# Inverting the softmax sums on Pool by a power of minus one, in place of DVE's reciprocal

## The chip, the cores and the metric

One core of a Trainium2 chip. The metric is the device time of one execution in microseconds (us), as the median of several runs.

Engine names are those of the profile: PE (matmul), PEld (weight load), DVE (VectorE), ACT (ScalarE), POOL (GpSimd), SP (the queue that issues the DMAs). L283 is line 283 of the kernel in question; the changed kernel's lines stand up to 5 higher than those of before.

## The reference

Attention with 32 inducing points over 4 batches of 12416 tokens of width 128, then a gated feed-forward layer (width 1536) on all 49664 tokens. Cut to what matters:

```python
def mab(q, kv):
    s = scale * (q @ kv.transpose(0, 2, 1))
    s = s - s.max(-1, keepdims=True)
    a = np.exp(s)
    a /= a.sum(-1, keepdims=True) + 1e-09      # the sums that the change inverts (second call)
    return a @ kv
h = mab(I, x)                                  # I: 32 inducing points
x = mab(x, h)                                  # each token: softmax over 32
...
ffn_out = gelu(x @ w_gate) * (x @ w_val) @ w_out
out = x + sigmoid(x @ w_res) * ffn_out
```

## The kernel before

Per batch there are 97 blocks of 128 tokens in 13 tiles of up to 8 blocks, and 25 token groups of 4 blocks (the last of 1). The exponentials of the second softmax lie in `e`, one block of 32 values per token, and their sums in `z`, a tile of up to 32 columns (one per block). Pool forms the sums, DVE inverts them, Pool multiplies to the normalised weights `a2`, and a DMA transposes these into `rt`, the right-hand side of all the products of that tile.

```python
p_sm = ... bufs=2                      # tag "a2": a ring of two buffers
p_fin ...                              # tags "th" and "at": rings of three, "fe": of two

def sums_b(b, j0, j1, eng):            # on Pool: halving additions in an a2 buffer
    t = p_sm.tile([P, PRE, Q, M], FP16, name="a2", tag="a2")...
    po.tensor_tensor(t[:, :w], ev[:, :, :M // 2], ev[:, :, M // 2:], AL.add)
    ...                                # three more halvings
    po.tensor_tensor(z.unsqueeze(2), t[:, :w, 0:1], t[:, :w, 1:2], AL.add)

def ones_b(b, j0, j1):
    z = e_of["z", b, t0][:, j0 - t0:j1 - t0]
    ve.reciprocal(z, z)

def weights_b(b, k, ...):
    a2 = p_sm.tile([P, PRE, Q, M], FP16, name="a2", tag="a2")
    eng.tensor_tensor(a2[:, :n], <e>, <z, broadcast>, AL.mult)
    sy.dma_start_transpose(rt, a2[:, :n]...)

def spread(b, c0, c1):                 # the next batch's first layer (h times w_gate, w_val), spread to hgv
    a2 = p_sm.tile([P, PRE, Q, M], BF16, name="a2", tag="a2")
    po.tensor_copy(a2[:, :n, 2 * s:2 * s + 2, :], hgt...)   # twice
    sy.dma_start_transpose(hgv_t[b]..., a2[:, :n]...)

def end(self, on_act):                 # the end of a token group
    if on_act:
        act.activation(fe, f, AC.Copy, bias=0.0, scale=1.0)
        po.tensor_tensor(th, th, fe, AL.mult)
        po.tensor_tensor(at, at, fe, AL.add)
    else:
        ve.scalar_tensor_tensor(th, th, 1.0, f, AL.add, AL.mult)
    po.tensor_tensor(at, at, th, AL.add)
    sy.dma_start(out[...], at)
```

The order in which all of this is queued stands in three tables of 25 rows, one row per token group: `plan_first`, `plan` (batches two and three) and `plan_last`. G is a half-slot of gates on PE and its gelu on ACT; V, Q, P a slot of values with none, one or two gates; a number the matmuls of the last layer; R and A the ACT instructions for `th` and `at`; E exponentials of the next batch, and behind the last of each block of 32 the sums; `o` a reciprocal; `l` one half of the next batch's first layer, after the second of which come the spread copies; a star an ending on ACT.

The softmax here doesn't subtract the row's maximum and nothing guards it: scores larger than these inputs give would overflow.

## Time and profile before

| | before |
|---|---|
| median of all its runs beside the changed kernel | 772.44 us (770.61 to 775.49, 6 runs) |
| ACT / DVE / PE busy, of a span of 770.5 us | 753.3 / 741.2 / 738.9 us |
| Pool busy | 467.4 us (61%) |
| reciprocals on DVE | 17, in sum 4.7 us |
| endings on ACT (fe) / on DVE (th) | 35 / 65 |

Three engines are nearly full, and Pool is at 61% only as an average. Between 77 and 116 us, where it also splits the next batch's input, it is busy for 35.5 of 39 us, and at the change to the third batch it works with hardly a gap from 380.6 to 397.1 us.

### The profile page before, as it was taken

To read this page: it belongs to the slowest core of one execution; us is meant where nothing else is said; L and a number is where in the kernel's file an instruction comes from. 1 tells how busy PE (TensorE), PEld (TensorE's weight loads), DVE (VectorE), ACT (ScalarE), POOL (GpSimd) and SP (SyncE) were. 2 spreads that over 40 slices of the span, in tenths; PEclk is the share of its full clock that TensorE was granted. 3 is DMA by queue.
4 is the path that set the end of the run, shared out by engine and by line. 5 is a ranking of instruction groups with operands and counts; after the bars stand their busy time and mean duration, and the time that the engine had idled before them with its cause. 6 is when DMAs were issued, how large, how long until landed. Compare 5 with 4: busy or idle time off the path is not lost.

```text
span 770.5 us, 23888 instructions
## 1 busy us (share of the span) xinstructions
PE 738.9 (96%) x9583; PEld 432.5 (56%) x9583; DVE 741.2 (96%) x735; ACT 753.3 (98%) x1506; POOL 467.4 (61%) x470
## 2 busy tenths in 40 slices
PE   6799999999999999999999999999999999999997
PEld 4455555565655655565655555556565555555555
DVE  7699999999999999989999999998999999999997
ACT  6899999999999999999999999999999999999997
POOL 0526988822787978923377797961367773443334
PEclk9889999999999999999999999999999999999999
DMA  8314589701055677521035496750105431110101
GB/s 340 124 45 129 134 191 188 165 30 43 31 119 110 157 176 192 141 46 43 29 65 112 112 210 154 139 150 29 39 21 128 87 88 43 42 43 29 42 30 60
DMA packets 118448, 78.15 MB, mean 101 GB/s; under 512 B 96672, under 2 KB 99392, under 8 KB 118336
## 3 DMA queue, kind: packets, MB, share of 16 engines
q1 hardware_dynamic: 118336, 76.62, 39.2%
q8 instruction: 75, 1.23, 0.7%
q14 instruction: 37, 0.30, 0.1%
HBM read 27.87 MB, written 25.43 MB: 69 GB/s over the span
## 4 chain that ended last, share of the span: by engine, by line
PE 47%; ACT 35%; issue 10%; DVE 4%; POOL 3%; DMA 1%; SPq 0%; ACTq 0%; DVEq 0%; POOLq 0%
ACT ge L368 23%; PE f L391 22%; PE g L357 12%; PE v L357 7%; PE g L399 3%; DVE u L362 3%; ACT at L410 3%; ACT th L405 3%; ACT e L166 2%; ACT fe L419 2%; ACT xt L141 1%; POOL lo L124 1%; ACT L166 1%; DMA xf<-in_x_dram 1%; DMA ge<-in_x_dram 1%
## 5 line engine op out<-in xcount | busy, mean ns | idle before, releaser
L362 DVE TENSOR_TENSOR u<-ge,v 128x1024 bf16<-128x1024 f32 x584 | 671.7, 1212 | 8.2 <-PE g L357 1.9
L368 ACT ACTIVATE ge<-g 128x512 f32<-128x512 f32 x1164 | 608.3, 661 | 2.7 <-PE g L357 1.6
L391 PEld LDWEIGHTS <-u 128*128 128x128 bf16 x4656 | 270.8, 98 | 206.3 <-issue 200.4
L391 PE MATMUL f<-wO,u 128*128 128x128 bf16 x4656 | 374.4, 221 | 4.0 <-DVE th L423 0.5
L357 PE MATMUL g<-rt,hgv 32*128 32x512 f16 x1152 | 337.7, 380 | 7.3 <-ACT ge L368 0.4
L357 PE MATMUL v<-rt,hgv 32*128 32x512 f16 x1152 | 222.3, 385 | 2.5 <-DVE u L362 1.5
L424 POOL TENSOR_TENSOR at<-at,th 128x512 f32<-128x512 f32 (+1 forms) x99 | 123.6, 1248 | 147.8 <-DVE th L423 66.1
L357 PEld LDWEIGHTS <-hgv 32*128 32x128 bf16 x2400 | 75.3, 91 | 87.8 <-issue 22.8
L420 POOL TENSOR_TENSOR th<-th,fe 128x512 f32<-128x512 f32 (+1 forms) x35 | 42.2, 1205 | 92.9 <-ACT fe L419 92.9
L294 POOL TENSOR_TENSOR a<-e,z 128x1024 f16<-128x1024 f32 (+1 forms) x48 | 89.8, 1880 | 5.7 <-DMA hgv<-a 5.4
L124 POOL TENSOR_TENSOR lo<-xf,hi 128x1024 f16<-128x1024 f32 x36 | 76.8, 2135 | 0.2
L399 PE MATMUL g<-hra,rt 128*128 128x128 f16 x768 | 72.1, 219 | 1.5
L410 ACT ACTIVATE at<-g 128x512 f32<-128x512 f32 (+1 forms) x100 | 65.0, 651 | 0.0
L405 ACT ACTIVATE th<-g 128x512 f32<-128x512 f32 (+1 forms) x100 | 64.3, 650 | 0.3 <-PE g L399 0.3
L399 PEld LDWEIGHTS <-rt 128*128 128x128 f16 x768 | 50.8, 98 | 12.4 <-issue 10.4
L423 DVE SCALAR_TENSOR_TENSOR th<-th,f 128x512 f32<-128x512 f32 (+1 forms) x65 | 44.1, 678 | 3.0 <-PE f L391 0.6
L118 POOL CAST hi<-xf 128x1024 f16<-128x1024 f32 x36 | 37.4, 1038 | 11.1 <-DMA xf<-in_x_dram 6.7
L421 POOL TENSOR_TENSOR at<-at,fe 128x512 f32<-128x512 f32 (+1 forms) x35 | 42.1, 1204 | 0.0
L162 PEld LDWEIGHTS <-xt 128*128 128x128 f16 x768 | 23.4, 97 | 7.2 <-issue 3.0
L166 ACT ACTIVATE e<-g 128x512 f32<-128x512 f32 (+3 forms) x40 | 20.4, 600 | 2.4 <-PE g L162 2.2
L419 ACT ACTIVATE fe<-f 128x512 f32<-128x512 f32 (+1 forms) x35 | 22.8, 650 | 0.0
L273 POOL TENSOR_TENSOR a<-a 128x256 f32<-128x256 f32 (+8 forms) x48 | 20.0, 416 | 3.8
(113 smaller groups left out, 261.0 us busy)
## 6 DMA issues: line engine op xcount, KB each, us to landing
out_dram<-at SPq DMA_DIRECT2D x96, 256.0 KB, 2.2
xf<-in_x_dram SPq DMA_DIRECT2D x38, 512.0 KB, 4.5
ge<-in_x_dram SPq DMA_DIRECT2D x10, 512.0 KB, 8.2
rt<-a SPq DMA_TRANSPOSE x48, 3.1
xt<-hi SPq DMA_TRANSPOSE x36, 4.2
ge<-in_moe_w_gate_dram SPq DMA_DIRECT2D x1, 512.0 KB, 9.3
ge<-in_moe_w_val_dram SPq DMA_DIRECT2D x1, 512.0 KB, 9.5
ge<-in_moe_w_out_dram SPq DMA_DIRECT2D x1, 512.0 KB, 4.9
```

What stands on the lines that cost most here:

```text
L124: eng.tensor_tensor(lo[:, :w, :P], xf_t.pop((b, k))[:, :w, :], hi_t[b, k][:, :w, :], AL.subtract)
L166: act.activation(e[:, (j0 - t0) * M:(j1 - t0) * M], bank[:, :(j1 - j0) * M], AC.Exp, bias=0.0, scale=scale)
L294: eng.tensor_tensor(a2[:, :n], ev[:, o:o + n, :].unsqueeze(2).to_broadcast([P, n, Q, M]), z[:, o:o + n].unsqueeze(2).unsqueeze(3).to_broad ...
L357: pe.matmul(*t[n], start=True, stop=True)
L362: ve.tensor_tensor(u[:, :n], ge_t.pop(value)[:, :n], v_t.pop(value)[:, :n], AL.mult)
L368: act.activation(ge_t[i][:, h * TOK:h * TOK + n], gb[:, :n], AC.Gelu, bias=0.0, scale=1.0)
L391: pe.matmul(self.ffn[:, k, :], u_t[self.gi, si][:, o:o + P], wO[:, fc, :], start=first, stop=not self.todo, skip_group_check=True)
L399: pe.matmul(bank[:, k * P:(k + 1) * P], rt_t[self.b, self.k][:, self.j0 + k, :], hra_t[self.b][:, s, :], start=True, stop=True)
L405: act.activation(self.th[:, :self.tw], self.mix(0), AC.Tanh, bias=0.0, scale=0.5)
L410: act.activation(self.at[:, :self.tw], self.mix(1), AC.Copy, bias=0.0, scale=1.0)
L423: ve.scalar_tensor_tensor(th, th, 1.0, f, AL.add, AL.mult)
L424: (ve if self.gi == ngrp - 1 else po).tensor_tensor(at, at, th, AL.add)
```

## The change

The intent is to take the reciprocals off DVE, one of the three full engines, and put them on Pool, the one with time left. The two earliest of the 17 stay on DVE. As Pool makes the sums itself, the inversion can follow at once and the `o` steps go from the tables. The tables were rearranged for that, so the change has two parts: the place of the inversion, and a new order of everything else.

```diff
-    def ones_b(b, j0, j1):
+    def ones_b(b, j0, j1, eng=po):
         z = e_of["z", b, t0][:, j0 - t0:j1 - t0]
-        ve.reciprocal(z, z)
+        if eng is ve:
+            ve.reciprocal(z, z)
+        else:
+            po.tensor_tensor(z, z, minus[:, :j1 - j0], AL.pow)
...
+    po.memset(minus, -1.0)
...
-                at(i, lambda j=j: sums_b(0, *j, po))
-                at(i + 6, lambda j=j: ones_b(0, *j))
+                at(i, lambda j=j: (sums_b(0, *j, po), ones_b(0, *j)))
...
                     sums_b(nb, j0 // WIDE * WIDE, j1, po)
+                    ones_b(nb, j0 // WIDE * WIDE, j1)
+                    inverted[nb] = j0 // WIDE * WIDE + WIDE
...   (the "o" step goes; all three tables are replaced; one row of each as an example)
-        "Q8G Q9 AGVr16 EEV VEEE2 EE11Q",
+        "RtQ2 GQ10A Qr20E EEV VEEEE 13P",
```

More of the change, by code (lines that the diff above doesn't have):

```diff
@@ L442 @@
     parts = konst.tile([P, 1], FP32, name="parts")
+    minus = konst.tile([P, WIDE], FP32, name="minus")
     sy.dma_start(ind_f, inducing)
@@ L522 @@
     sums_b(0, 0, half, ve)
-    ones_b(0, 0, half)
+    ones_b(0, 0, half, ve)
     sums_b(0, half, WIDE, po)
@@ L532 @@
     first_layer(0, TOK)
-    ones_b(0, half, WIDE)
+    ones_b(0, half, WIDE, ve)
     weights_b(0, 0, half, PRE)
@@ L562 @@
     plan_first = [
-        "GGGP P5 P6 QG6G Q4 GQR7",
-        "P 6P8 RA6P A6P7G Q7 V",
-        "GG7GGV 8GQ8GR 5P G5QG 7P 7P",
-        "5P R8GVG7GG VA9 PGG8 P 8Q",
-        "G7QG 6A6Q G6PG 7P GQ8A 5P9",
-        "P9 P10RR 7Q P6 GG7QG 7QG8G",
-        "Q9R P7 A4GV P7 GG7Q G7GVG5",
-        "P 7GQ6A4R5 P G4GVG 6P6 A5GQ7G",
-        "Q7 GGV6G G7GVG VGR8 GGVA7G GVG6",
-        "QR4 GVG1 G6QG 5P5 A6P VG",
-        "R12A3P9G Q7 GGV17 EEV VE15 P17",
-        "QG7 PR9 AP6G Q6 P6 GGQ6",
-        "P7G V G6GP7R 4GP7 P7 P7 *",
@@ L576 @@
-        "P3 A8GQ7 P8 P1c P2 4RGVA",
-        "9GVG8 GQ8 GQ9 AR8GQ G7P 7GGV",
-        "5P5 A6P 7P5R 6P cP10 P3A11G",
-        "Q7 P5R 7Q G5QE EV4E 19EV *",
-        "cP11G Q8 GVG5A 1cGQ6R 3P 7GQ8",
-        "GQ8 GVG8AR 8V GP7GG 6Q G6GVG",
-        "7P7 GG6P8R 1GhQG P7G G4tP Q10A",
-        "QR8 Qr11EE V VE2 EE2E4EP Qo21",
-        "6P 5P 6QG3A 7lAP 5P7 GVG7G",
-        "Q7 R4P 7GQ8 A3lP Q8R G4P6 *",
-        "GQ7G Q7Ro oo4P 12GQ G13GVG9A P7G",
-        "Q9 P10G *",
+        "GGGQ P PG7 GQ5G VG8 R2QG",
@@ new lines @@
+        "5GQ 6P 7AGQ 8RPG 7GQ7 AQ6 *",
+        "1RQ4A 4P7 P12 GP 6Q6 P5R",
+        "6GQ 6QG7 GQ7GG 5GVGA5 P3G Q6",
+        "P7 P9 RP6 P4A 8P P",
+        "8R2GQ 7GQ4A7 P7 GVG8G G5VG P7GG7",
+        "P6G Q7G Q7 GQ 7GG7GQ Q7RR9",
+        "P4 4P8 GGV9AA 7GP7G GV7 PG",
+        "7P7 QG7 GQ7G G6PA7 QG6 P7",
+        "P4 R5P 6P2R4 7AP V6GG 8QG8",
+        "A3P7G Q8 P2 6Q EEV16E Q6 *",
+        "P17 3Q 4Q R2cP 5P8 RP7",
+        "P8 P7 P5 A8AP 2P 9GQ10 *",
+        "P5 R9GQ 13P cP GGV7 R4P7",
+        "QG7 P9 A2P 7R5AP 6P 6P",
@@ L588 @@
+        "6P7 GQ7 GVGR 8V GG8AP Q",
+        "G7RG4GV G6GQ7G GV3A 8VG G7P5 1QEEE29",
+        "EcP19R GVG4 GQ 6Pc GQ7 P6A",
+        "3P6 P6 QG7GG 3Q QA8 GG7GQ",
+        "7P 9RQR 8P9 AGhVGG2G Q8G Q8Gt",
+        "Q14E EEV VE1E EE15GV P21GG V6",
+        "PR8G Q6 P5 AG2Q QR9G G6P7",
+        "GQ8 P5 lQ5R A8lP6 GQ8 GQ7G",
+        "Q3A 10P7A 7rP3 P8G Q1 G7GV",
+        "G8GQ 6R7P8GG *",
     ]
     plan = [
-        "VA GVGR3 GP9 GP 9QG 5QA *",
-        "7QR7 R2P 6P6 Q6 AP13 P5",
-        "A5Q G7GQ 7P7 GG4V GRVG6GG6 P7 *",
@@ L593 @@
-        "GQ7A Q5 P6 RQ11G P12G Q7",
-        "VGG7 P9 GQ9G G4Q VG A14RP *",
-        "12P 9GQ13R P9 QA 9GQ 7GQ",
-        "5P 9RQG 9AGGVG 3P7 P7 GGV",
-        "9RQG8G Q6 P3 A5P VGG8GG6 P8 *",
-        "P7 P7 GQ6 A6GQ V G12GVG7",
-        "GGV6G 1GQ8 RP 7P 7P GQA7",
-        "R6P 8P 10GQ7 R2A8VG GGQ7 GQ8A *",
-        "4P 6P 6GGV 7RGV10GG Q14 P8",
-        "P8 P8 P4 A6GVG P7R4G Q5R *",
-        "6V GG7GVG7G Q1 11AP 12GQ 7GV",
-        "G7P 7GVG8RA7G GQ6 GQ7 GVG 7GQ",
-        "7GVG 7AQ13E 1EEV6 EEE7EcP 3cPG V3R8G",
@@ L606 @@
-        "Q7G Q7GG 7GV P8R A6P 6GQ3 *",
-        "A8P 6P7R Q3 GGV1 cP8G Q9A",
-        "5GV G7GQ 7GVG12 GGcGVGGhR2G V1 P8",
-        "GG7QG 7P7 P7 RA9GP6 tGV1G1 GQ7G",
-        "Q8G Q9 AGVr16 EEV VEEE2 EE11Q",
-        "P26G VR8l 1GP 6GV G6P7GG V5oA",
-        "6Q G4R7P2G 5lP 3P7 GQ7G oQ7",
-        "RA8P7R3Go Q4 G2Q P6oG G7P6A5 QG8G",
-        "Q 8P8G *",
+        "Q6 P2 VRRA 4AP3 5P 6P",
+        "8P6 P7G VG5 GG8RP 5P7 GVG7",
+        "GVG1 6GQ7G QA9A 6RQ P3G 4P *",
+        "8AQR 8P6 P7 GQ12 GQ G12GVG6 *",
@@ new lines @@
+        "QG7G Q6R 5P 12VGG VG12 2A3P10",
+        "GVG9 P8 GG4V GVGR8G G5GQ 6P7",
+        "GQ7G Q7 RA8GVG A5P6 P6 P7 *",
+        "GVG 7GQ8R Q 9P G13GGV4 3GQ *",
+        "8AQ A8P 12P Q8G QG6 P6",
+        "GGV6A4 P5 GQ R5QG 8RPG6 P9",
+        "GVG8 GQ8G Q9A R8GGQ 6P 7GQ *",
+        "7GVG6G Q6 GVG8A 8QG GV8G G1Q6",
+        "P3 A8P 6P5 GQ5R 6V GGP8A",
+        "6GVG11G Q12R3G Q8 GGP6G Q8G Q",
+        "8GVG6R7G Q8 R5GGQ V2 A9GGV G8GVG",
+        "8GQ 21EEEV VEEE7 EcP3c GP V7GG",
+        "6P 7P 8RQ A10RP Q7GG3 3P7",
@@ L615 @@
+        "GV G7GGV 6P 8RA7PcG Q8G Q5",
+        "A7P8 GVG8 GQ12GGc GVG2 P7GG V6",
+        "A5Q G5RhGVG P7 GQ8 AR8GP6 GQ10",
+        "RtQ2 GQ10A Qr20E EEV VEEEE 13P",
+        "Q15 13P5 l2P GV5l A6QG5R 5GQ",
+        "7P7 P8 A5RP Q7G G6QG 7GV",
+        "G6V GA7P8 GG7GV VGG7GG7 GQ 6P6",
+        "R5P8 P9GG *",
     ]
     plan_last = [
-        "VGGR4G Q QA8G P8 GQ5 1P6G *",
-        "Q4G RQ6 P4 3AQ 3GQ 8P *",
-        "R12VG G7P 7GQ8 RQ A14PG6 Q7",
-        "GQ8G V G9GQ10RA 8AP 6P 7P6 *",
-        "P4R6 P2 5P 12P Q10A P3R *",
@@ L622 @@
-        "6P5 P6 P6 P 12AP 7Q *",
-        "5P A8GQ 6P 6P3R 7Q 6PG12",
-        "P7 QG7 QG3 R8QG 8A3P Q7G *",
-        "G8P7 P7 P7G Q12A VGG11 2GQ4 *",
-        "3P6 RGV8 GQ14A P3 6P 6P7",
-        "P7 P8 RP 6A5GP5 QR7 P7 *",
-        "P 8P 8GQ 13PR 11P6 P *",
-        "7P8 AGV4 GVG12AGG V12 P7 GQ6",
-        "GQ5 2P 8RR8PG6 VG G6QG VG *",
-        "A8RQ G7P 7P7 Q7A QG14 GVG",
-        "8P6 GGV3 A9P 8GGGV P11 R3P *",
-        "8P7G QG6 1P 12P Q9 1RP *",
-        "5AQ 8P 11QGA9 5Q P10R 6P",
-        "7P 7VGG 6GQ 7GR5PG GQ 8GQ",
@@ L636 @@
-        "9P11G Q4 5GQ 6A5VGG VGG4R 4P10",
-        "AVG G7P 7QG9 AR7Q GQ5GGG V8 *",
-        "AQG9G Q12 RP6 Q8 GP9 P9 *",
-        "P10GG V 9GQ8 R3Q GQ15 VGG10 *",
-        "P10 P11 A2P Q17 P11 P6",
-        "GGPRGG5GGAG1 8P",
+        "Q V7RA 5GP 11GVG P7A P *",
+        "6QG 6GVG 8RGP V10A P8 P7",
+        "GQ7 P4R8 P7G QG7G P VA4 *",
+        "R10P 11GQ10 P7 6AP 8Q R7P",
+        "7P 5P7 P2R 5A7Q P7 GG7GQ *",
+        "6QG8 P3 5GQ 12GQ R9P4A VG2",
+        "5VGG 6P10 QG8 AR4PG 5QG 7GQ",
+        "8P9 P3 R9P 7P P9 AGVG *",
@@ new lines @@
+        "R9P 6P9 P15 P A9P P4 *",
+        "GVA8 QG 8QG 7GV G12GGQ 12GQ6 *",
+        "P8R QG Q9 AQG4 3VG6 RP *",
+        "14P 10P10 GGV12 2PG6 Q 5P7",
+        "P7R 3P 8Q G4A8P P5A 7P",
+        "10P12R 2P7R1 4Q P6G G5P 6V *",
+        "GG10AP 9P 7Q5 GVGR12 P6 P4G *",
+        "GV3G VGA9 GP2 4P 8Q P10",
+        "P8A 3P 4P7 GQ8RR 8P Q8",
+        "GG7Q G6P 5P2 A10P 10RP Q8 *",
+        "AR6P 7P 8P 7GQ 12PA 12GQ7 *",
+        "GVG 7P8 R1QG3 Q10 PG13 QG8 *",
+        "GQ8 Q G10AVG 9GP 7Q7 VGG9",
@@ L642 @@
+        "R3P 9GQ5 A8PR 2P 6P5 GQ3A *",
+        "8P6 GGV6G QA 12Q P13 P4R *",
+        "10P 8P 13PG5 Q 9GQ 14PR",
+        "V10 A10GPGGGGGGGG *",
     ]
@@ L706, in background @@
         cuts = [0, 24, 48, 72, nblk]
-        todo = {"E": [], "l": [], "c": [], "o": []}
+        todo = {"E": [], "l": [], "c": []}
         for kind in "ab":
@@ L711, in background @@
         todo["c"] = list(zip(cuts, cuts[1:]))
-        todo["o"] = list(range(0, nblk, WIDE))
         todo["l"] = [0, 1]
@@ L733, in step @@
                 res_layer(nb)
-            elif t == "o":
-                t0 = todo["o"].pop(0)
-                ones_b(nb, t0, min(t0 + WIDE, nblk))
-                inverted[nb] = t0 + WIDE
         return step
```

## The prediction

> **What bounds the kernel now.** I read the page's totals first, then the costliest groups, then the list of waits, then engine by engine the busy time of seven stretches, and last Pool's timeline at the change from one batch to the next.
>
> ```profile
> span 770.5 us, 23888 instructions
> PE 738.9 (96%) x9583; PEld 432.5 (56%) x9583; DVE 741.2 (96%) x735; ACT 753.3 (98%) x1506; POOL 467.4 (61%) x470
> ```
>
> Three engines are full at once. ACT is fullest: it is idle for 17 us of 770.5. PE and DVE are idle for about 30 us each. Pool has some 300 us to spare in sum.
>
> ```profile
> 0.00:36.00 36.00, 24.88 (x505) 18.25 (x506) 26.01 (x46) 26.85 (x43) 9.79 (x33) 0.95 0.65 246
> 36.00:161.00 125.00, 121.53 (x1449) 67.32 (x1447) 122.43 (x118) 123.24 (x247) 89.36 (x85) 0.97 0.58 134
> 161.00:343.00 182.00, 178.75 (x2388) 105.02 (x2384) 176.85 (x173) 181.81 (x365) 125.97 (x123) 1.00 0.45 109
> 385.00:766.00 381.00, 371.92 (x4625) 215.87 (x4622) 374.82 (x357) 379.77 (x772) 227.38 (x214) 1.00 0.33 81
> ```
>
> The columns are stretch, length, then busy us of PE, weight loads, DVE, ACT, Pool. ACT loses 9.2 us before 36 us (waiting for the input) and 4.5 us after its last instruction at 766. Only about 3.6 us of ACT's idle time lies in the 730 us between. So in the middle the time is the sum of ACT's work, with DVE a few us behind; in the last batch DVE is level with ACT (both full between 693 and 732 us).
>
> ```profile
> L362 DVE TENSOR_TENSOR u<-ge,v 128x1024 bf16<-128x1024 f32 x584 | 671.7, 1212 | 8.2 <-PE g L357 1.9
> L368 ACT ACTIVATE ge<-g 128x512 f32<-128x512 f32 x1164 | 608.3, 661 | 2.7 <-PE g L357 1.6
> L423 DVE SCALAR_TENSOR_TENSOR th<-th,f 128x512 f32<-128x512 f32 (+1 forms) x65 | 44.1, 678 | 3.0 <-PE f L391 0.6
> L419 ACT ACTIVATE fe<-f 128x512 f32<-128x512 f32 (+1 forms) x35 | 22.8, 650 | 0.0
> L280 DVE RECIPROCAL z<-z 128x32 f32<-128x32 f32 (+3 forms) x17 | 4.7, 285 | 0.5 <-POOL z L275 0.4
> ```
>
> The first two groups are the work that cannot change. The other three are what this change touches: each of 100 token groups ends either with one DVE instruction (65 of them) or with an ACT copy and two extra Pool instructions (35). And all reciprocals together are 4.7 us of DVE, 0.6% of the span.
>
> **What the Trainium skill says.** "Perfetto Trace Analysis", Per-engine timelines: a DVE or ACT record runs until the write is acknowledged, and for GPSIMD it advises start-to-start spacing. The trace agrees that records overlap: the ge activations last 661 ns but pass at 608.3/1164 = 0.52 us each. So I count every term below by spacing. "VectorE: DVE Perf Modes", First, the fixed hardware budget: the reciprocal is an iterative divide with a repeat count of 8. Here 128x32 takes 345 ns and 128x1 106 ns: 239 ns for 31 elements, 7.7 ns or 7.4 cycles of 0.96 GHz each; it agrees. "GPSIMD Engine Reference", Elementwise — side-by-side cycle accounting: about 2.6 cycles per element for two inputs, and with many operations per element about 3 operations per cycle. The additions of 512 elements are spaced 1.24 us here; 512 x 2.6 / 1.2 GHz = 1.11 us plus dispatch, so it agrees. No page gives the cost of a power on GPSIMD, and no instruction in this trace is one. The same page, Key points, warns of contention when DVE reads two SBUF inputs; DVE's u takes one input from PSUM, and its mean is 1215 ns where Pool is busy (77 to 116 us, Pool 35.5 of 39) and 1217 ns where it is not (693 to 732, Pool 13.9 of 39). So more Pool work should not slow DVE.
>
> **The change part by part.** *Reciprocals.* 15 of 17 leave DVE: 11 of 128x32 and 4 of 128x1. Their spacing:
>
> ```profile
> 397.85 0.35 DVE L280 RECIPROCAL z<-z 128x32 f32<-128x32 f32 x1
> 398.11 2.28 DVE L362 TENSOR_TENSOR u<-ge,v 128x1024 bf16<-128x1024 f32 x2
> ...
> 404.61 0.16 DVE L280 RECIPROCAL z<-z 128x1 f32<-128x1 f32 x1
> 404.68 1.20 DVE L362 TENSOR_TENSOR u<-ge,v 128x1024 bf16<-128x1024 f32 x1
> ```
>
> 0.27 us and 0.07 us: 11 x 0.27 + 4 x 0.07 = 3.2 us off DVE.
>
> *Tables.* By count of the two programs' instructions, ACT copies fe go from 35 to 30 and DVE's th from 65 to 70. All else is equal in number (1164 ge, 584 u, the same matmuls). One fe is spaced 0.48 to 0.52 us, so ACT loses 5 x 0.5 = 2.5 us of work. One th is spaced 0.60 us (401.75 to 402.35), so DVE gains 5 x 0.6 = 3.0 us. DVE's sum is therefore 3.0 - 3.2 = -0.2 us: what the reciprocals gave up is spent on relieving ACT. Pool loses 10 instructions of 1.24 us = 12.4 us.
>
> By batch: the first keeps 4 ACT endings, so there ACT gains nothing and DVE loses 7 reciprocals (1.5 us). Batches two and three go from 8 to 6 each: ACT -1.0 us each, DVE +0.3. The last goes from 15 to 14: ACT -0.5, DVE +0.6, where DVE is just as full. So I credit ACT with the full 2.0 us in the middle batches and with nothing in the first and last, plus about 0.2 us that a new order may save of the 3.6 us of inner idle time. Sum: -2.2 us.
>
> *Powers on Pool.* 15 are added, each directly behind its sums. As cheap as an addition of that size one would be 0.20 us (383.65 to 383.85 in the fence below). I assume 60 to 100 basic operations per element for a power in software; at the skill's 3 operations a cycle that is 20 to 33 cycles, and 32 elements at 1.2 GHz take 0.5 to 0.9 us, with 0.2 us around it 0.7 to 1.1 us. That is an estimate; I take p = 0.9 us. In sum 11 x 0.9 + 4 x 0.25 = 11 us, which the 12.4 us that leave Pool pay for. What counts is where they stand: three large and one small between the last exponentials of a batch and the first weights of the next.
>
> ```profile
> 380.58 1.28 POOL L270 TENSOR_TENSOR a<-e 128x512 f32<-128x512 f32 x1
> 381.94 1.63 POOL L273 TENSOR_TENSOR a<-a 128x256 f32<-128x256 f32 x3
> 383.65 0.24 POOL L275 TENSOR_TENSOR z<-a 128x32 f32<-128x32 f32 x1
> 383.85 1.29 POOL L270 TENSOR_TENSOR a<-e 128x512 f32<-128x512 f32 x1
> ...
> 391.68 1.27 POOL L424 TENSOR_TENSOR at<-at,th 128x512 f32<-128x512 f32 x1
> 392.91 1.90 POOL L294 TENSOR_TENSOR a<-e,z 128x1024 f16<-128x1024 f32 x1
> ...
> 399.27 0.74 POOL L242 COPY a<-hgt 128x256 bf16<-128x256 bf16 x2 [2.13 <-DMA rt<-a]
> 401.22 1.90 POOL L294 TENSOR_TENSOR a<-e,z 128x1024 f16<-128x1024 f32 x1 [1.20 <-DMA hgv<-a]
> ```
>
> Pool works without a gap from 380.6 to 397.1 us here. The spread weights hgv land at 401.2, and PE first uses them for the next batch at about 404.3: 3.1 us of room. In the changed program the two spread copies stand ahead of the first weights in the second and third of the three transitions. There the copies would start at 391.7 + 1.2 = 392.9 and end at 394.8, and the first weights, of 1.9 us, end at 396.7; their transpose lands some 3.3 us later at 400.0, all plus 3p + 0.25. The room is 4.3 us. In the first transition the order is as before: there hgv landed at 217.1 and was used at 220.8 (3.7 us), Pool idled 0.9 us on the way, and the exponentials now stand about 1 us of ACT work earlier: 5.5 us. With p = 0.9 each transition uses 3 us. They fit, so the powers cost nothing on the path.
>
> **The rivals.**
> First, *a slow power*. If its operations form a chain whose latency is not hidden, at 4 cycles each ("fp32 dependent chain", the same GPSIMD page, Performance pitfalls for Q7 kernels), 60 x 4 x 32 / 1.2 GHz = 6.4 us. Then each transition is late by 3 x 6.4 + 0.25 - 4.5 = 15 us, PE and with it ACT and DVE starve, and the kernel is some 45 us longer, 815 us. The break-even is near p = 1.4 us; a loss of 2% (15.4 us) with the 2.2 us gained needs 17.6 / 3 = 5.9 us per transition, p of about 3.4 us. For it: no line of this trace shows such an instruction. Against it: Pool's other simple operations run at the documented rate, and the tables were rearranged around it with no more distance given than 1 to 2 us.
> Second, *DVE is the bound*. The waits say ACT waited 2 us for PE and DVE 8 us in its main group, and in the last batch DVE is full. If DVE set the time throughout, -0.2 us is all there is: 772 us, the same.
> Third, *the order of the new tables is worth more than the counts*. All 75 rows differ. It can return at most the 3.6 us of inner ACT idle time beyond the 2.5 us: 766 us. Or it wins the estimate of a model and loses on the chip by a few us: 775 us. The wait list shows no stall above 1 us on PE in the steady part, which speaks for a kernel with little left to find.
>
> **Range and chances.** 772.2 - 2.2 = 770.0 us. Low end: all of ACT's 2.5 us and most of its idle time, 767. High end: a power of about 2 us, three late transitions of 6.25 - 4.5 = 1.8 us, less good order: 778. Faster by 2% (756.8) would need 15 us from ACT, which has no such time to give: 1%. Slower by 2% is the slow power, which I give 10%. The rest, 89%, is the same within 2%.
>
> **What would show it.** The group of powers on Pool, 11 of 128x32, spaced about 0.9 us; DVE's group of reciprocals down to 2 and th up to 70; fe down to 30; ACT's busy sum near 750.8 and DVE's near 741. Pool's wait for hgv in the transitions should remain, and PE should show no wait on a transpose of weights or of hgv. I am wrong if PE's first product of a batch waits for one of these DMAs for several us, if the powers take over 1.5 us, if u slows beside them, or if ACT's sum falls and its inner idle time grows by as much.

## The result, and the profile after

| | before | after |
|---|---|---|
| median | 772.44 us | 826.5 us (824.62 to 830.11, 6 runs) |
| ratio | | 1.0703, 95% interval 1.0671 to 1.0735 |
| span of the profiled run | 770.5 us | 823.7 us |

The changed kernel is 7% slower. First the totals of its page and three of its groups (columns: busy us, mean ns of one; then idle time just before, with its main releaser):

```profile
span 823.7 us, 23897 instructions
PE 748.0 (91%) x9582; PEld 437.9 (53%) x9583; DVE 741.9 (90%) x725; ACT 753.8 (92%) x1501; POOL 517.6 (63%) x476
...
L413 ACT ACTIVATE at<-g 128x512 f32<-128x512 f32 (+1 forms) x100 | 64.1, 649 | 32.3 <-DMA out_dram<-at 30.1
...
L426 DVE SCALAR_TENSOR_TENSOR th<-th,f 128x512 f32<-128x512 f32 x70 | 47.5, 678 | 30.2 <-PE f L394 29.1
L283 POOL TENSOR_TENSOR z<-z,minus 128x32 f32<-128x32 f32 (+1 forms) x15 | 62.1, 4140 | 1.2
```

ACT and DVE are busy for as long as before, to within a microsecond, so for these two the 53 us are idle time. PE is busy 9 us longer (738.9 to 748.0) and idle for the rest; why it is slower for a while is shown below. The last line is the new one: 15 powers are 62.1 us. The mean mixes two shapes. In the timeline of Pool at the first change of batch they come apart (columns: start us, duration us):

```profile
202.36 5.45 POOL L283 TENSOR_TENSOR z<-z,minus 128x32 f32<-128x32 f32 x1
207.76 1.30 POOL L270 TENSOR_TENSOR a<-e 128x512 f32<-128x512 f32 x1
...
211.17 5.44 POOL L283 TENSOR_TENSOR z<-z,minus 128x32 f32<-128x32 f32 x1
...
219.95 5.44 POOL L283 TENSOR_TENSOR z<-z,minus 128x32 f32<-128x32 f32 x1
...
226.75 0.56 POOL L283 TENSOR_TENSOR z<-z,minus 128x1 f32<-128x1 f32 x1
227.28 2.48 POOL L427 TENSOR_TENSOR at<-at,th 128x512 f32<-128x512 f32 x2
```

The duration is real and not an artefact of the record: the addition behind the first power starts at 207.76, 5.40 us after the power did. And directly behind the last power stand two final additions of token groups, which had been waiting in Pool's queue. In ACT's timeline of the same time:

```profile
214.80 0.62 ACT L371 ACTIVATE ge<-g 128x512 f32<-128x512 f32 x1
228.57 0.60 ACT L408 ACTIVATE th<-g 128x512 f32<-128x512 f32 x1 [13.16 <-POOL at L427]
```

ACT stops for 13.2 us. It wants to write the next `th`, the ring of three is full, and what frees one is the final addition at 227.28. There are three such stops, one per change of batch. In the other two it is `at`, which waits for the output DMA that such an addition precedes. At the second change:

```profile
432.67 0.60 ACT L413 ACTIVATE at<-g 128x512 f32<-128x512 f32 x1 [13.45 <-DMA out_dram<-at]
```

The stretches of 2 us around the first stop show a second cost (columns: length, then busy us of PE, PEld, DVE, ACT, POOL, then the granted PE clock as a share of full speed, the DMA share and GB/s):

```profile
214.00:216.00 2.00, 2.00 (x43) 1.74 (x39) 2.00 (x3) 1.42 (x4) 2.00 (x1) 1.00 0.03 8
...
222.00:224.00 2.00, 0.00 (x0) 0.00 (x0) 0.00 (x0) 0.00 (x0) 2.00 (x1) 0.50 0.00 0
...
232.00:234.00 2.00, 2.00 (x21) 1.17 (x18) 1.71 (x2) 1.57 (x4) 1.95 (x3) 0.50 0.63 119
...
236.00:238.00 2.00, 1.88 (x23) 1.13 (x23) 1.91 (x3) 1.97 (x6) 0.51 (x1) 1.00 0.63 122
```

PE's clock falls to half during the stop and is still at half from 230 to 234, when PE is busy again. There PE is full and ACT, which normally is, is not (1.57 of 2). The Trainium skill's "TensorE: Matmul & The Clock Gate" (What's actually happening) states this: half clock after at least one idle window of about 3.4 us, full clock after at least one busy window of that length. The trace agrees in kind; here PE worked again from 229.2 and the clock came back at about 234.3, 5.1 us later. After the other two stops, of the same length, it took longer: PE worked again from 433.3 and 633.8, and the clock came back at about 442.5 and 643.9, 9.2 and 10.1 us later.

To say where the time went I use marks that every kernel here has: the starts of the ACT table loads for the exponentials. "Change 1" runs from the mark ahead of the second exponentials of batch two to the first ones of batch three, and so on; each of the three holds one change of batch. "Start" is all up to the first of these marks and so holds the first batch, with its three powers. The two stretches left out differ by 0.3 us at most.

| us longer than the run with multiplications (below) | start | change 1 | change 2 | change 3 and the rest |
|---|---|---|---|---|
| before | 0.8 | -1.3 | 0.9 | 0.3 |
| after | 4.8 | 14.9 | 16.4 | 17.2 |

### The profile page after: what moved, and what is told of

Its sections match the earlier page's. It is cut to its first block, busy times and chain, and to the rows that moved or that the text cites. A ratio compares the mean times of both kernels' runs of the same rounds, so it can differ in the third digit from the quotient of the medians. Undisturbed runs are those within 1.5% of the kernel's fastest.

```text
span 823.7 us, 23897 instructions
## 1 busy us (share of the span) xinstructions
PE 748.0 (91%) x9582; PEld 437.9 (53%) x9583; DVE 741.9 (90%) x725; ACT 753.8 (92%) x1501; POOL 517.6 (63%) x476
## 4 chain that ended last, share of the span: by engine, by line
PE 34%; ACT 32%; POOL 15%; issue 10%; DVE 5%; DMA 3%; SPq 0%; ACTq 0%; DVEq 0%; POOLq 0%
ACT ge L371 22%; PE f L394 15%; PE g L360 9%; POOL z L283 7%; PE v L360 5%; DVE u L365 4%; ACT th L408 3%; ACT at L413 3%; PE g L402 2%; POOL a L273 2%; POOL a L270 2%; POOL lo L124 1%; POOL at L427 1%; DMA out_dram<-at 1%; ACT xt L141 1%
## 5 line engine op out<-in xcount | busy, mean ns | idle before, releaser
L365 DVE TENSOR_TENSOR u<-ge,v 128x1024 bf16<-128x1024 f32 x584 | 671.0, 1212 | 34.6 <-PE g L360 20.7
L394 PEld LDWEIGHTS <-u 128*128 128x128 bf16 x4656 | 274.4, 99 | 211.9 <-issue 207.3
L408 ACT ACTIVATE th<-g 128x512 f32<-128x512 f32 (+1 forms) x100 | 63.9, 645 | 13.5 <-POOL at L427 13.2
L423 POOL TENSOR_TENSOR th<-th,fe 128x512 f32<-128x512 f32 (+1 forms) x30 | 35.7, 1192 | 62.7 <-ACT fe L422 62.7
L426 DVE SCALAR_TENSOR_TENSOR th<-th,f 128x512 f32<-128x512 f32 x70 | 47.5, 678 | 30.2 <-PE f L394 29.1
L283 POOL TENSOR_TENSOR z<-z,minus 128x32 f32<-128x32 f32 (+1 forms) x15 | 62.1, 4140 | 1.2
L402 PEld LDWEIGHTS <-rt 128*128 128x128 f16 x768 | 51.9, 98 | 12.5 <-issue 10.5
L424 POOL TENSOR_TENSOR at<-at,fe 128x512 f32<-128x512 f32 (+1 forms) x30 | 35.8, 1193 | 0.0
L166 ACT ACTIVATE e<-g 128x512 f32<-128x512 f32 (+3 forms) x40 | 20.3, 600 | 2.1 <-PE g L162 2.0
```

Source lines behind the costliest of these rows:

```text
L283: po.tensor_tensor(z, z, minus[:, :j1 - j0], AL.pow)
L365: ve.tensor_tensor(u[:, :n], ge_t.pop(value)[:, :n], v_t.pop(value)[:, :n], AL.mult)
L394: pe.matmul(self.ffn[:, k, :], u_t[self.gi, si][:, o:o + P], wO[:, fc, :], start=first, stop=not self.todo, skip_group_check=True)
L402: pe.matmul(bank[:, k * P:(k + 1) * P], rt_t[self.b, self.k][:, self.j0 + k, :], hra_t[self.b][:, s, :], start=True, stop=True)
L408: act.activation(self.th[:, :self.tw], self.mix(0), AC.Tanh, bias=0.0, scale=0.5)
```

## The experiments

Twelve kernels were run. "Correct" means equal to the reference within its tolerance.

### 1. The same program with a cheap instruction in the place of the power: mult

```diff
-            po.tensor_tensor(z, z, minus[:, :j1 - j0], AL.pow)
+            po.tensor_tensor(z, z, minus[:, :j1 - j0], AL.mult)
...
-    po.memset(minus, -1.0)
+    po.memset(minus, 1.0 / 1024.0)
```

> The changed kernel, with each of the 15 powers on Pool turned into a multiplication of the same shape by 1/1024 (a wrong but plausible number: the sums are near 32). Order of all instructions unchanged. Theory 1, the power's own duration of 5.44 us blocks Pool's queue: the instruction falls to about 0.24 us, the four stalls go, and the time is 768 to 772 us. Theory 2, the rearranged tables lose by themselves (their order or fewer ACT endings): the time stays above 790 us. Theory 3, more instructions on Pool disturb DVE[...]: not much changes either, above 790 us, since the number of Pool instructions is the same.

Measured: 771.97 us, before 772.04, ratio 0.9992 (0.9966 to 1.0018). It even passes as correct, as the sums lie so near 32.

```profile
span 770.4 us, 23898 instructions
PE 737.7 (96%) x9583; PEld 432.2 (56%) x9583; DVE 740.6 (96%) x725; ACT 751.6 (98%) x1501; POOL 460.9 (60%) x476
...
L283 POOL TENSOR_TENSOR z<-z,minus 128x32 f32<-128x32 f32 (+1 forms) x15 | 3.6, 237 | 1.2
```

All of the loss is the duration of the power: 62.1 us become 3.6, and the stops are gone: no wait of ACT for Pool or for an output DMA is left in the list of its waits, and those for PE in its main group come to (columns: us in total, times, longest us)

```profile
ACT ge L371 <- PE g L360: 1.6, 5, 0.6
```

Theories 2 and 3 fall. The run shows one thing more. With an inversion that costs almost nothing on Pool, and with five ACT endings fewer, the kernel is as fast as before and, as far as the runs can tell, no faster: the interval leaves room for a gain of 0.3% (2.6 us) at most. So this is about all that the change could have brought.

### 2. How much power the changes of batch can hide: dose8, dose16, dose4

Only the first 8, 16 or 4 columns of each block go through the power, the others through the multiplication (wrong, though within the tolerance).

```diff
-            po.tensor_tensor(z, z, minus[:, :j1 - j0], AL.pow)
+            n = min(4, j1 - j0)                      # or 8, or 16
+            po.tensor_tensor(z[:, :n], z[:, :n], minus[:, :n], AL.pow)
+            if j1 - j0 > n:
+                po.tensor_tensor(z[:, n:], z[:, n:], tiny[:, :j1 - j0 - n], AL.mult)
...
+    po.memset(tiny, 1.0 / 1024.0)
```

> The changed kernel, with the power applied to the first 8 columns of each block only and a multiplication for the other 24 (wrong on purpose). The power should take about 0.56 + 7 x 0.157 = 1.7 us, with the multiplication 1.9 us per block, 5.7 us per transition. If the room of 4.3 to 5.5 us per transition worked out in the prediction is right, each transition is late by about 1 us or less: 770 to 774 us. If there is no room at all, each of 3 transitions costs its 5.7 us: 785 us or more.

> As the run before with 16 columns by the power: about 0.56 + 15 x 0.157 = 2.9 us, 3.1 us with the multiplication, 9.4 us per transition. With room of about 5 us, 4.4 us late in each of three transitions and little in the first batch: about 783 us. If the loss is in proportion to the power's length with no threshold, half of the 54 us: about 797 us.

> The changed kernel, with the power for the first 4 columns of each block and a multiplication by 1/1024 for the rest: about 1.28 us per block in place of the 0.25 us of the multiplication alone, 3.1 us more per transition. The runs with 8, 16 and 32 columns lost 5.5, 8.9 and 16.2 us per transition for 4.9, 8.8 and 15.9 us more power, while the waits recorded on ACT were about 3 us shorter than the power and the granted clock was near 0.5 for some us after each stop. Theory A, a room of about 3 us, then a wait, and a restart at a lowered clock that costs some 3 us: 3.1 us just fit, no stop, no restart, 772 to 774 us. Theory B, no room at all, every us of power lengthens the kernel: about 781 us.

| columns of power | one power, us | median | ratio to before (95%) | start | change 1 | change 2 | change 3 |
|---|---|---|---|---|---|---|---|
| 4 | 1.02 | 783.04 us | 1.0141 (1.0125 to 1.0157) | -0.6 | 0.8 | 4.0 | 6.7 |
| 8 | 1.65 | 788.44 us | 1.0207 (1.0179 to 1.0236) | -0.9 | 3.7 | 5.9 | 6.8 |
| 16 | 2.91 | 801.6 us | 1.0374 (1.0344 to 1.0405) | 4.0 | 7.6 | 8.6 | 10.5 |
| 32 (the change) | 5.44 | 826.5 us | 1.0703 (1.0671 to 1.0735) | 4.8 | 14.9 | 16.4 | 17.2 |

(The last four columns are us longer than mult, by the marks.) The power goes from 0.56 us for one column to 5.44 us for 32: 157 ns per column, or 189 cycles at the 1.2 GHz that the skill gives for this engine ("GPSIMD Engine Reference", Specifications). All three expectations that counted on a room (4.3 to 5.5 us, about 5, about 3) failed. Even 3.1 us of power per change of batch cost 11 us in sum, which is what theory B (no room at all) said of the time. The columns are finer than theory B, though: change 1 hides the 3.1 us but for 0.8, while changes 2 and 3 hide nothing. These are the two in which the new tables put the spread copies ahead of the first weights. Pool's timeline at change 2, in mult and then in dose4:

```profile
394.93 1.85 POOL L242 COPY a<-hgt 128x512 bf16<-128x512 bf16 x4
399.57 1.90 POOL L297 TENSOR_TENSOR a<-e,z 128x1024 f16<-128x1024 f32 x1 [2.78 <-DMA hgv<-a]
```

```profile
398.41 1.84 POOL L242 COPY a<-hgt 128x512 bf16<-128x512 bf16 x4
402.95 1.90 POOL L300 TENSOR_TENSOR a<-e,z 128x1024 f16<-128x1024 f32 x1 [2.71 <-DMA hgv<-a]
...
408.11 0.39 PE L363 MATMUL g<-rt,hgv 32*128 32x512 f16 x2 [1.81 <-DMA rt<-a]
```

Between the spread copies and the first weights Pool waits 2.8 us: both take their scratch from the ring of two `a2` buffers, and the weights need one that the hgv transposes have read. So the weights come 2.8 us later than the prediction had them, and in dose4 the first product of the next batch waits for their transpose (last line). Change 1 is different: there the weights stand ahead of the copies, and what ends the room is the output ring. In dose8 ACT waits 2.4 us there for a final addition on Pool, of the 3.7 us lost.

### 3. Taking that wait away: dose4_own, and its controls mult_own and after_own

```diff
-        a2 = p_sm.tile([P, PRE, Q, M], BF16, name="a2", tag="a2")
+        a2 = p_fin.tile([P, TOK], FP32, name="fe", tag="fe", bufs=2).bitcast(BF16).rearrange(
+            "p (j q m) -> p j q m", q=Q, m=M)
         for s in range(2):
```

> The run with 4 columns of power (783 us), with one edit: the scratch of the spread copies no longer comes from the ring of two a2 buffers that the sums and the weights use, but from the ring of fe buffers, which is idle there. In the run with the multiplication Pool waited 2.8 us for the hgv transposes between the spread and the first weights, because of this ring; the prediction had let the weights start at once. Theory E, this wait used up the room (4.3 us worked out less 2.8 is about 1.5, and what was measured is near 0.6): without it the first weights come 2.8 us earlier and the 11 us lost fall to 1 to 4 us, 773 to 776 us. If the transposes themselves, or the output ring, take up the room: no change, 781 to 784 us.

> The control for the two runs above: multiplication in place of the power, and the scratch of the spread from the fe ring. Nothing waited there, so no gain: 771 to 773 us.

> The changed kernel with the full power and the same edit. Theory E: about 2.8 us less late weights in the second and third transition, but the stops there were at the output ring (at waits for its output), before the weights are missed, so little is gained: 820 to 827 us. If the weights were what set the length of the stop: about 818 us or less.

Measured: dose4_own 775.23 us, ratio 1.0031 (1.0002 to 1.0061); mult_own 771.22 us, 0.9977 (0.9957 to 0.9997); after_own 824.44 us, 1.0666 (1.0638 to 1.0693). In dose4_own the weights follow the copies at once:

```profile
398.83 1.85 POOL L243 COPY fe<-hgt 128x512 bf16<-128x512 bf16 x4
400.64 1.90 POOL L301 TENSOR_TENSOR a<-e,z 128x1024 f16<-128x1024 f32 x1
```

Of the 11 us that the short power cost, 8 come back, and changes 2 and 3 cost 1.0 and 1.8 us in place of 4.0 and 6.7. Theory E holds: the wait for the ring had used up the room. The controls show the rest. Without a power the edit moves the median by 0.1% (mult 771.97, mult_own 771.22), which is less than the width of the intervals, and with the full power by only 2 us. There the kernel still stops at the output ring, before it misses the weights; in after_own at the second change:

```profile
434.66 0.60 ACT L414 ACTIVATE at<-g 128x512 f32<-128x512 f32 x1 [13.45 <-DMA out_dram<-at]
```

### 4. Is the output ring what makes the stop? tail_dve

A ring of four for `th` or `at` does not build: the pool would need 18 KB per partition, and 16.2 are left. Instead the final additions of the five groups that end near a change of batch go to DVE, so that they no longer stand behind the powers.

```diff
-            (ve if self.gi == ngrp - 1 else po).tensor_tensor(at, at, th, AL.add)
+            on_ve = self.gi == ngrp - 1 or (self.gi < 3 * gpb and self.gi % gpb in (19, 20, 21, 22, 23))
+            (ve if on_ve else po).tensor_tensor(at, at, th, AL.add)
```

> The changed kernel with the powers as they are, but the final addition of the five token groups that end around each batch change (at plus th) on DVE in place of Pool. Theory 4, the stall comes from the ring of three th and three at buffers, which Pool's queue releases only behind the powers: the waits of th and at for Pool or for the output DMA in the three transitions go, the rest of the lateness is that of the spread weights and the first weights, 2 to 6 us each, and the time falls from 826 to 795 to 806 us. Theory 5, as the prediction's rival had it, the stall is that of the next batch's weights and of hgv alone: the time stays at 822 to 828 us.

Measured: 827.46 us, ratio 1.0706 (1.0671 to 1.0741), correct: no change. But the waits are others. The longest of after and of tail_dve (columns: us in total, times, longest us):

```profile
ACT at L413 <- DMA out_dram<-at: 30.1, 4, 13.4
...
ACT th L408 <- POOL at L427: 13.2, 1, 13.2
```

```profile
ACT ge L371 <- PE g L360: 41.9, 33, 13.2
...
PE g L360 <- DMA rt<-a: 24.8, 2, 12.9
```

The waits for the ring in the three changes are gone, so theory 4 is right about what stops ACT in the changed kernel. Its number is wrong, and theory 5's number is right: at the second and third change the stop moved to the transposed weights and is as long (PE waits 11.9 and 12.9 us for them). At the first change the longest stop is only 4.9 us, for hgv, and yet by the marks 13.5 us are lost there; that remainder was not taken apart. Both things, the output and the next weights, stand behind the same burst of sums and powers on Pool. Freeing one of them lets ACT run on only until it misses the other. The run has a side effect without a control: the 15 moved additions are 12.8 us more work on DVE, which is full too (204 to 210 us: 6.00 of 6), and this can hide a gain of some us.

### 5. The same powers at other places: oldtab, lazy, lazy_paced

oldtab is the kernel before with the power on Pool where DVE had the reciprocal, each some slots after its sums. lazy is the changed kernel in which each tile of weights inverts its own 8 columns just ahead of its multiplication; lazy_paced also queues these tiles farther apart. All three are correct.

```diff
 (oldtab, to the kernel before)
-        ve.reciprocal(z, z)
+        if first_ones:                      # the two earliest
+            ve.reciprocal(z, z)
+        else:
+            po.tensor_tensor(z, z, minus[:, :j1 - j0], AL.pow)
 (lazy, to the changed kernel)
+        if b > 0 or t0 > 0:
+            po.tensor_tensor(z[:, o:o + n], z[:, o:o + n], minus[:, :n], AL.pow)
-                at(i, lambda j=j: (sums_b(0, *j, po), ones_b(0, *j)))
+                at(i, lambda j=j: sums_b(0, *j, po))
-                    ones_b(nb, j0 // WIDE * WIDE, j1)
 (lazy_paced, on top)
-                at(133 + (7 * i) // 2, lambda i=i: due.append((nb, i)))
+                at(133 + 5 * i, lambda i=i: due.append((nb, i)))
```

> The kernel before with its own tables, and the 15 reciprocals done by the power on Pool at the places where DVE had them. There one power, not four, stands ahead of the spread copies of hgv, and the others come between tiles of weights. Theory C (place in the queue): a delay of 5.2 us against a room of 3 us in each transition, and a restart, so about 5 us each, and some us in the first batch: 785 to 795 us. If the position did not matter: about 826 us.

> The changed kernel, correct, with the same power work but at other places: each weights tile inverts its own 8 columns just ahead of its multiplication (1.65 us), so no power stands between the sums and the first weights; some 80 us of power in all against 62. Theory C, what costs is the place in Pool's queue: the stops in the transitions go, and the time is 772 to 786 us, where the upper end is a backlog, since Pool now has about 61 us of work in the 52 us in which 13 tiles of weights are queued. Theory D, the total work on Pool costs: the time is above 826 us.

> As the run before, and the weights tiles queued one per 5 slots in place of 3.5, so that Pool has room for the power beside each. Theory C: no backlog, 771 to 776 us. Theory D: above 826 us, as the total work is that of the run before.

| | power on Pool, sum | median | ratio to before (95%) |
|---|---|---|---|
| after | 62.1 us | 826.5 us | 1.0703 (1.0671 to 1.0735) |
| oldtab | 61.9 us | 806.47 us | 1.0437 (1.0414 to 1.046) |
| lazy | 74.7 us | 794.16 us | 1.0285 (1.0258 to 1.0312) |
| lazy_paced | 74.7 us | 803.11 us | 1.0404 (1.0384 to 1.0424) |

More power on Pool with less loss: the place in the queue decides, not the sum, and theory D falls. The sizes that I expected of theory C were all too good. In lazy the longest waits are again for the output ring:

```profile
ACT at L415 <- DMA out_dram<-at: 15.7, 10, 4.2
```

The later ones are only 0.4 to 2.5 us each, but there are 4.2 us at 116 us and 2.7 us at 163 us, in the first batch, where Pool had little time left to begin with (38.3 busy of 39 us between 77 and 116, against 35.5 before). lazy_paced moved weights into the stretch where Pool splits the next input, and its longest stops, of 5.9 and 5.5 us, are at 306 and 500 us. In the last batch no further input has to be split, and there it hides its powers: by the marks changes 1 and 2 lose 11.0 and 10.8 us, and change 3 loses nothing (-0.4 us), with 13 powers of 20.3 us in sum on Pool. No order that I tried hides them in all batches.

### 6. What the reciprocals were worth on DVE: norecip

The kernel before, with its 15 late reciprocals left out (wrong).

```diff
-        ve.reciprocal(z, z)
+        if first_ones:
+            ve.reciprocal(z, z)
```

> The kernel before with its 15 late reciprocals simply left out (wrong result on purpose), tables as before. This is the most that taking them off DVE could ever bring with the old tables. If DVE's 3.2 us lay on the path: 769 us. If ACT and the order of the tables set the time, as the prediction holds: 771.5 to 773 us.

Measured: 771.25 us, before 772.57, ratio 0.9981 (0.9961 to 1.0002). DVE's busy sum falls from 741.2 to 738.6 us, and the time by 1.3 us by the medians, with an interval that just touches no gain at all. So even inversion for nothing would have been worth about 0.2%, and 0.4% at most.

## Why the prediction was wrong, point by point

- **What bounds the kernel, and the counts** held: reciprocals on DVE fell to 2, th rose to 70, fe fell to 30, DVE's u kept its mean of 1212 ns over the kernel, and beside the first power of the first change (202 to 208 us) its median was 1214.
- **The gain of 2.2 us** did not show even without the power: mult has 1.7 us less of ACT work (753.3 to 751.6) and the same time. By the marks, only change 2 is shorter (0.9 us, where 1.0 was credited), and change 1 is 1.3 us longer. Runs of one kernel spread over more than this, and mult's interval (0.9966 to 1.0018) includes a gain of 2.2 us as well as none, so it stays open whether any of it is real.
- **The term that failed first is the duration of the power**, p = 0.9 us, estimated from 60 to 100 operations at 3 per cycle. It is 5.44 us: 189 cycles per column and not 20 to 33. The rival "a slow power", with 4 cycles for each of 60 operations and 6.4 us, was near the truth, and its 15 us per change of batch are close to what the marks show (14.9, 16.4, 17.2). That closeness is partly luck: with the measured 5.44 us its own sum gives 3 x 5.44 + 0.25 - 4.5 = 12.1 us, so a power too long made up for a room too large. Why a power takes 189 cycles no run shows. The rival was given 10%. That weight was the mistake in judgment: I took a routine that no trace had shown at its best rate.
- **The room of 4.3 to 5.5 us per change of batch** failed too, and would have made even p = 0.9 visible: dose4, at 1.02 us plus the multiplication, lost 11 us. For the second and third change the step let the first weights start at the end of the spread copies. They wait another 2.8 us for an `a2` buffer, and the last line of the prediction's own Pool fence, "[1.20 <-DMA hgv<-a]", was this wait; at the first change of the kernel before it was 2.69 us (217.07). dose4_own, which takes it away, loses 3 us. For the first change the output ring ended the room (experiment 2).
- **Where the stop would show.** The prediction looked for PE waiting for transposes of hgv or weights. In the changed kernel ACT stops earlier, at the rings of `th` and `at`, which the prediction did not consider at all; tail_dve shows that, at the second and third change, the predicted stop lies right behind.
- **Two costs were left out.** The first batch has three powers too, in a stretch where Pool is full (4.8 us). And a stop of several us halves PE's clock for some us after it. Its share was not measured by itself; what the three changes lost (48.5 us) less the three stops recorded on ACT (13.2, 13.4 and 13.4, together 40 us) is 8.5 us, an estimate that holds this and the other small waits after a restart. Of these, ACT's idle time between each restart and the return of the full clock is 1.1, 2.0 and 3.1 us, 6.2 in sum, and part of that is a wait for transposed weights (1.1 us at the third). By change the remainders are 1.7, 3.0 and 3.8 us, in the order of the stretches at half clock (5.1, 9.2, 10.1 us).
- **A reading that was off, with nothing resting on it:** 106 ns is the shortest of the four reciprocals of 128x1 that were moved; their mean is 144, and that of 128x32 is 342. That is 6.4 ns or 6.1 cycles per element and not 7.4, so the agreement with the skill's count of 8 is looser than the prediction says.

## What to carry to other kernels

Moving work to an engine that is 61% busy is free only where its queue has time (lazy_paced hides its powers in the last batch and in no other): look at how busy it is in the stretch in question, and at what stands behind the new instruction in its in-order queue. Work out the room from a wait that the trace shows, buffer rings included, and not from the end of the instruction before. When an instruction's duration is known from no trace, measure it by itself before weighing anything by it, and first ask what its removal is worth: here leaving it out altogether brought about 0.2%, with no gain still inside the interval.

## What the Trainium skill lacked or had wrong

- "GPSIMD Engine Reference" gives no cost for a power. A tensor_tensor power in fp32 on 128 partitions took 0.56 us for 1 column, 1.02 for 4, 1.65 for 8, 2.91 for 16 and 5.44 for 32: 157 ns per column, 189 cycles at its 1.2 GHz. Its figure of about 2.6 cycles per element of two-input work (Elementwise — side-by-side cycle accounting) is that of an addition and no guide to a power, which took over 70 times that; the multiplication of 128x32 took 0.25 us.
- "TensorE: Matmul & The Clock Gate" (What's actually happening) gives at least one busy window of about 3.4 us until full clock. After stops of 13 us the clock here stayed at 0.50 for 5.1, 9.2 and 10.1 us from PE's first matmul. This does not contradict "at least one", but how busy PE must be in a window is not said there, and no run here tests it.
- Nothing to mend: "GPSIMD Engine Reference" (Key points), on contention with DVE, names instructions in a 2-port mode or with two SBUF inputs. u, with one input from PSUM, had a mean of 1212 ns before and after.
